# Seven products for more of the first MLP layer, and an own order for each chunk, in a fused attention and MLP kernel

## The chip, the cores and the metric

The kernel runs on one core of a Trainium2 chip. The metric is the device time of one execution in microseconds; the kernel before has a median of 330.25 us over three runs (330.21 to 332.17). The engines are called as the profile calls them: PE (TensorE, matmul), PEld (its weight loads), DVE (VectorE), ACT (ScalarE), POOL (GpSimd) and SP (SyncE, which issues DMAs). Each engine works through its own queue in program order; semaphores order the queues among themselves.

## The reference, cut to what matters

Attention with a forgetting gate over 8 batches, 8 heads, 576 positions and head size 64, and then an MLP of two layers with a tanh GELU over all 4608 rows.

```python
scores = scale * np.matmul(q, k.transpose(0, 1, 3, 2))
log_f = np.log(np.clip(f, 0.0001, 1.0))
cum = np.cumsum(log_f, axis=-1)
decay = cum[:, :, :, None] - cum[:, :, None, :]
scores = np.where(causal, -1000000000.0, scores + decay)
attn = np.exp(scores - max)          # then divided by its row sum
attn_out = np.matmul(attn, v)        # (8, 8, 576, 64)
x = attn_out.transpose(0, 2, 1, 3).reshape(4608, 512)
h = x @ w_in                         # 512 -> 2048
g = gelu_tanh(h)
out = g @ w_out                      # 2048 -> 512, float32
```

## The kernel before, in words

The 64 pairs of batch and head are worked in 16 "quads" of four heads. The 4608 rows of the MLP are worked in 9 "chunks" of 512 rows (0 to 8). The attention of a quad runs while an MLP chunk runs: chunk c is played together with the attention of the quads 2c+2, 2c+3 and the first part of 2c+4.

The order is written out by hand in tables of words. `SETUP` and `FRONT` are the first part of the program, up to chunk 1; `TABLES[c]` (from line 87) is the order within chunk c from chunk 2 on. `play(c)` goes through the words and calls the function behind each, and every function issues its instructions to the engines' queues at once. So a table sets, for each engine, the order of its queue. `q3` in a table means quad 2c+3, and so on. The words that matter here:

- `P.pr` (`mlp_in`, L369 and L376): one pair of 128 hidden features in full: 8 matmuls of 512 columns into one tile of PSUM, then one GELU of 1024 elements a partition on ACT. `P.pr.1` uses the tile `psO` of the attention, the others one of the two tiles of `psS`. Eight pairs make a chunk's first layer.
- `R.k` (`seven_in`, from L407): unit k, which stands for the pairs k and 4+k, in seven products of half size instead of eight (28 matmuls of 256 columns). It is called three times (R, R, R), which issue five products, one and one. It uses both `psS` tiles and both `psM` banks. Per unit DVE does one copy out of PSUM (L432) and five additions (L423), each with one operand in PSUM, and ACT does four GELUs of 512 elements (L428). Before, only the chunks 7 and 8 use it, for the units 1 and 3.
- `T` (`x_sums`, L390): four subtractions of 128x512 bf16 on DVE, both operands in SBUF, that make t1, t2, t4, t3 out of the next chunk's x; `R` multiplies with them. `K.k.n` (`w_sums`, L405): the same kind of sums of the weights for unit k, four in all, made once. Their results lie in the columns of x (`xT`) of a chunk that is done with (`HOMES`).
- `F.n`, `f.n` (`seven_products`, L504): the next n matmuls of the chunk's second layer, itself in seven products of 16 matmuls of 256 columns; `f` issues each as four matmuls of 32 columns of the array. After matmul 16 and 48 ACT copies a result (L525); after 32, 64, 80, 96 and 112 DVE adds (L529). `O.512` issues what is left of the chunk before.
- `G.half.which` (`gelu_sums`, L483 to L489): sums of the GELU's results for those seven products, 128x1024 bf16 on DVE, both operands in SBUF. Two of them (3 and 4 of half 1) are always issued after matmul 32.
- `S.i.r` (L256, L264): scores of quad i, round r, and their exponentials, two of 1024 elements a partition on ACT. They need both tiles of `psS`. `M.i.r` (L270): the causal mask on them, `affine_select` on POOL. `D.i` (L324, L343 to L347): row sums and their reciprocals on DVE. `V.i.x` (L324, L355): half of attention times v into `psO`, and DVE's product with the reciprocals into `xT`.
- `VW.i` (L210): v times the gate's weights, 128x1280, on POOL, both operands in SBUF. `CL.i` (L215): a small copy of it on DVE.
- `TK.i`, `TQ.i` (L193): transposes of k and q on DVE. `LK.i`, `LQ.i` (L187): their loads, issued by POOL. `LV` (L164): the load of v for the batch after next, issued by SP.
- `X`, `Y` (L224, L228): a tiny activation that makes ACT load the table for Exp or for GELU.

PSUM is full: `psS` has two tiles of two banks, `psM` two of one, `psO` one of two.

The few lines on which the steps rest:

```python
# line 387: t1, t2, t4, t3 of x, in this order
todo = ((t1, b12, b11), (t2, b22, t1), (t4, b21, t2), (t3, b22, b12))
# line 430: the first call of a unit
multiply(pa, a11, b11, True)      # then DVE copies pa
multiply(pb, s2, t2, True)        # each next one: DVE adds
multiply(pc, s1, t1, True)
multiply(pd, s3, t3, True)
multiply(pa, a12, b21, False)
```

Of the kernel before, what the change touches and what calls it, by code (L numbers as in the profile page):

```python
# [16 lines left out]
def kernel(  # L17
# [53 lines left out]
    """  # L71

    FRONT = """
        TQ.0 B.2.256 TK.1 SB TR LP.2@LQ.0 B.2.128 CW S.0.0 B.5.384 B.1.256 Z TQ.1 vw.0.0 S.0.2 WI.0 LQ.2 M.0.0 B.3.384 H.1.0.1
        LP.3 B.1.256 vw.1.0 WI.1@LU.4 W H.1.1.1 WI.3 B.2.256 WI.2 H.1.0.0 M.1.0.1 D.0.0 M.1.0.0 H.0.1.1 V.0.0.0 H.0.1.0 B.2.256 M.0.1 H.1.1.0 V.0.1.0
        D.1.0 H.0.3.0 B.2.128 V.1.0.0 LX.1.1 H.0.3.1 V.1.1.0 m.0.3.2 H.1.3.0 m.0.3.4 B.1.256 VW.1.1 H.1.3.1 B.4.128 vw.0.1 D.0.1 M.1.3 S.1.2 M.1.1 LK.2
        V.0.1.1 V.0.0.1 WO.0 J.0.1 D.1.1 J.0.0 WO.1@LV.1.1 V.1.1.1 V.1.0.1 J.0.3 WO.2@WI.1 VW.3 J.1.0 WO.3 LK.3 LQ.3 J.1.1 TQ.2 J.1.3 LQ.4
        LX.1.0@WO.2 TK.2 J.0.2 J.1.2 X LK.4 F.0.6 TK.3 B.3.256 S.2.0 LK.5 F.0.9 S.2.2 F.0.10 S.2.1 TQ.3 TQ.4 F.0.10 LV.2.0@LK.5 m.2.1 vw.2
        TK.4 S.3.0 f.0.1 M.2.2 CL.2 LQ.5 M.2.0 D.2 f.0.6 S.3.1 m.3.0 F.0.6 V.2.0 S.3.2 TK.5 LK.6 M.3.2 f.0.7 V.2.1 CL.3
        S.4.1 m.3.1 LQ.6 F.0.6 TQ.5 H.4.2.1 D.3 H.4.0.1 LQ.7 VW.4 H.4.0.0 V.3.1 v.3.0 f.0.3 H.4.2.0 CL.4 I.1.0 m.4.1 U.0 LV.2.1@LQ.5 I.1.4  # L80
        TQ.6 m.4.2.3 I.1.1 I.1.5 U.1 LV.3.0@LQ.7 m.4.2.2 TK.6 G.0 M.4.0 I.1.2 I.1.3 U.3 I.1.6 I.1.7 G.1.1.2 U.2 X F.1.14 S.5.0 f.1.28 S.5.1 D.4 M.5.0 f.1.16
        S.5.2 V.4.0 m.5.2.3 f.1.10 VW.5 V.4.1 CL.5 m.5.2.2 LQ.8 S.6.0 f.1.10 M.5.1 D.5 f.1.7 S.6.1 V.5.1 f.1.12 V.5.0 vw.6 S.6.2
# [39 lines left out]
    def many(n, shape, dtype, name):  # L122
        return [singles.tile(shape, dtype, name=f"{name}{i}") for i in range(n)]
# [11 lines left out]
    vw = many(2, [128, NT + 1, 4, D], BF16, "vw")  # L135
# [256 lines left out]
    def w_blocks(k):

        n = 256
        a11, a12, a21, a22 = (w_in_sb[:, 2 * b:2 * b + 2, HU * a + n * k:HU * a + n * (k + 1)]
                              for a in range(2) for b in range(2))
        old = xT[:, :, CH * HOMES[k]:CH * (HOMES[k] + 1)]
        return a11, a12, a21, a22, old[:, 0:2, 0:n], old[:, 0:2, n:], old[:, 2:4, 0:n]

    def w_sums(k, eng, which):  # L400

        a11, a12, a21, a22, s1, s2, s4 = w_blocks(k)
        todo = ((s1, a21, a22), (s2, s1, a11), (s4, a12, s2), (a21, a11, a21))
        for n in which or range(4):
            (eng.tensor_sub if n else eng.tensor_add)(*todo[n])  # L405

    def seven_in(c, k):  # L407

        a11, a12, s3, a22, s1, s2, s4 = w_blocks(k)
        b11, b12, b21, b22, t1, t2, t3, t4 = x_blocks(c)  # L410
        pa, pb = (psS.tile([128, 2, 512], FP32, name="ps_ab", tag="s")[:, 0].rearrange("p (j n) -> p j n", j=2) for _ in range(2))
        pc, pd = (psM.tile([128, 2, HC], FP32, name="ps_cd", tag="m") for _ in range(2))

        def multiply(ps, w, x, first):
            for j in range(2):
                for dt in range(2):
                    nc.tensor.matmul(ps[:, j], w[:, dt, 128 * j:128 * j + 128], x[:, dt],  # L417
                                     start=(first and j == 0 and dt == 0), stop=(dt == 1),
                                     skip_group_check=True)

        def add(ps, y, pool, tag):
            st = pool.tile([128, 2, HC], FP32, name="h_st", tag=tag)
            nc.vector.tensor_add(st, ps, y)  # L423
# [8 lines left out]
        nc.vector.tensor_copy(p1, pa)  # L432
# [226 lines left out]
    def load_values(b, half):  # L659
# [58 lines left out]
    def quads(call):  # L718
# [61 lines left out]
```

## Time and profile before

| | |
|---|---|
| median of three runs | 330.25 us |
| profiled execution: its span, the one time given of it | 328.4 us |
| median less that span | 1.85 us |
| PE busy | 316.9 us (96%) |
| DVE busy | 206.4 us (63%) |
| ACT busy | 201.7 us (61%) |
| POOL busy | 110.6 us (34%) |
| first `P` of chunk 2, 3, 4, 5 on PE at | 102.26, 137.11, 171.59, 206.06 us |
| first `P` of chunk 6, 7, 8 on PE at | 240.54, 273.40, 299.14 us |

All times in a view of the trace are microseconds from the start of the span. A row of the timeline gives the start, the time that the merged instructions took, the engine, the line, the operation, what it writes and reads, and how many were merged; in brackets stands how long the engine was idle before and who ended that. PE was granted its full clock throughout (1.00 in every stretch asked for).

A full 512-column matmul is shown with 379 ns, but that is from its issue to its modelled end; matmuls overlap. The 64 of a chunk's first layer fill 13.82 us, so one takes 0.216 us of PE.

### The profile page before, as it was taken

How to read it: one execution, taken by the hardware profiler on the slowest of the kernel's cores; microseconds unless marked ns; L12 is line 12 of the kernel's file. 1: busy time of each engine (PE TensorE's matmuls, PEld its weight loads, DVE VectorE, ACT ScalarE, POOL GpSimd, SP SyncE). 2: the span in 40 equal slices, each digit the busy share in tenths (PEclk: the TensorE clock that was granted, in tenths of full speed). 3: DMA queues.
4: the chain of work that ended last, by engine and by line, in shares of the span. 5: the costliest groups of instructions: out<-in, count | busy, mean ns of one | idle time of the engine just before them, and what ended most of it. 6: DMA issues, size and time to landing. Idle time of an engine off the chain costs nothing.

```text
span 328.4 us, 11961 instructions
## 1 busy us (share of the span) xinstructions
PE 316.9 (96%) x5421; PEld 206.5 (63%) x5421; DVE 206.4 (63%) x323; ACT 201.7 (61%) x231; POOL 110.6 (34%) x155
## 2 busy tenths in 40 slices
PE   3999999999999999999999999999999999999995
PEld 1458844545776477646774577557754777787684
DVE  4686039884887865674567456636553767875772
ACT  4685576866767586668656775768675841721630
POOL 8985572510504415520544054303440140000000
PEclk9999999999999999999999999999999999999999
DMA  7999999861124990295129711761110102002012
GB/s 123 210 214 215 168 230 199 167 165 24 36 40 94 236 208 31 94 187 108 37 68 182 140 37 36 160 122 36 36 66 0 36 21 81 2 32 98 0 35 96
DMA packets 44323, 33.42 MB, mean 102 GB/s; under 512 B 27488, under 2 KB 37856, under 8 KB 44272
## 3 DMA queue, kind: packets, MB, share of 16 engines
q0 software_dynamic: 8848, 16.58, 28.0%
q1 hardware_dynamic: 35280, 16.01, 18.4%
q8 instruction: 42, 0.69, 0.9%
q14 instruction: 9, 0.07, 0.1%
q10 hardware_dynamic: 144, 0.07, 0.1%
HBM read 36.85 MB, written 9.44 MB: 141 GB/s over the span
## 4 chain that ended last, share of the span: by engine, by line
PE 86%; DMA 3%; DVE 3%; ACT 3%; POOL 2%; issue 2%; POOLq 0%; DVEq 0%; ACTq 0%
PE ps_h L369 29%; PE ps_w L504 25%; PE po L324 9%; PE ps_s L256 8%; PE pso L574 4%; PE ps_h L458 4%; DMA v_nat<-in_v_dram 2%; PE ps_cd L417 2%; ACT pt L264 2%; PE ps_ab L417 2%; PE po_m L310 1%; POOL vw L210 1%; DMA out_dram<-o_st 1%; POOL v_nat L164 0%; PE ps_o L324 0%
## 5 line engine op out<-in xcount | busy, mean ns | idle before, releaser
L264 ACT ACTIVATE pt<-ps_s 128x1024 bf16<-128x1024 f32 (+2 forms) x100 | 93.7, 988 | 39.4 <-PE ps_s L256 34.9
L369 PE MATMUL ps_h<-xT,w_in_sb 128*128 128x512 bf16 x448 | 99.0, 379 | 0.0
L376 ACT ACTIVATE gT<-ps_h 128x1024 bf16<-128x1024 f32 x56 | 57.2, 1022 | 49.9 <-PE ps_h L369 48.3
L270 POOL TENSOR_SCALAR_AFFINE_SELECT pt<-pt 128x512 bf16<-128x512 bf16 (+3 forms) x65 | 38.2, 597 | 132.9 <-ACT pt L264 131.8
L369 PEld LDWEIGHTS <-w_in_sb 128*128 128x128 bf16 x448 | 43.8, 98 | 50.1 <-issue 0.4
L504 PEld LDWEIGHTS <-gT 128*32 128x32 bf16 (+1 forms) x1253 | 50.9, 97 | 6.4 <-issue 1.7
L504 PE MATMUL ps_w<-w_out_sb,gT 128*32 128x256 bf16 (+1 forms) x1056 | 46.9, 273 | 0.0
L504 PEld LDWEIGHTS <-gsum 128*32 128x32 bf16 (+1 forms) x1256 | 38.9, 97 | 2.7 <-issue 1.4
L256 PE MATMUL ps_s<-qT,kT 32*128 32x64 bf16 (+5 forms) x896 | 36.8, 263 | 0.3 <-ACT pt L264 0.2
L483 DVE TENSOR_TENSOR gsum<-gT 128x1024 bf16<-128x1024 bf16 x16 | 11.0, 689 | 35.2 <-ACT gT L376 35.2
L504 PE MATMUL ps_w<-usum,gsum 128*32 128x256 bf16 (+1 forms) x832 | 30.7, 273 | 1.0 <-ACT snap L525 0.7
L355 DVE TENSOR_TENSOR xT<-po,rb 128x576 bf16<-128x576 f32 x26 | 19.6, 755 | 18.9 <-PE po L324 18.6
L193 DVE STREAM_TRANSPOSE kT<-k_c 128x576 f32<-128x576 f32 x16 | 20.0, 1247 | 17.8 <-DMA k_c<-in_k_dram 17.8
L210 POOL TENSOR_TENSOR vw<-v_nat,wT 128x1280 bf16<-128x1280 f32 (+1 forms) x13 | 30.4, 2338 | 0.1
L529 DVE TENSOR_TENSOR o_st<-ps_w,snap 128x512 f32<-128x512 f32 x31 | 21.3, 689 | 13.2 <-PE ps_w L504 11.8
L256 PEld LDWEIGHTS <-kT 32*128 32x128 bf16 x896 | 16.9, 93 | 17.4 <-issue 12.6
L324 PE MATMUL po<-pt,vw 128*32 128x64 bf16 (+4 forms) x624 | 22.5, 279 | 0.0
L324 PEld LDWEIGHTS <-vw 128*32 128x32 bf16 x672 | 14.3, 96 | 10.6 <-issue 3.7
L193 DVE STREAM_TRANSPOSE qT<-q_c 128x576 f32<-128x576 f32 x16 | 19.9, 1242 | 1.1 <-PE ps_s L256 0.5
L164 POOL DMA_DIRECT2D v_nat<-in_v_dram x20 | 15.3, 776 | 4.6 <-DMA w_out_sb<-in_moe_w_out_dram 4.6
L504 PE MATMUL ps_w<-usum,gT 128*128 128x256 bf16 (+1 forms) x197 | 16.4, 273 | 0.0
L574 PE MATMUL pso<-w_out_sb,gT 128*32 128x512 bf16 (+1 forms) x115 | 15.6, 380 | 0.0
(97 smaller groups left out, 327.0 us busy)
## 6 DMA issues: line engine op xcount, KB each, us to landing
out_dram<-o_st SPq DMA_DIRECT2D x35, 256.0 KB, 2.4
k_c<-in_k_dram POOLq DMA_DIRECT2D x16, 288.0 KB, 5.8
q_c<-in_q_dram POOLq DMA_DIRECT2D x16, 288.0 KB, 7.3
v_nat<-in_v_dram SPq DMA_DIRECT2D x16, 256.0 KB, 8.5
w_in_sb<-in_moe_w_in_dram POOLq DMA_DIRECT2D x4, 512.0 KB, 9.5
w_out_sb<-in_moe_w_out_dram POOLq DMA_DIRECT2D x4, 512.0 KB, 8.3
v_nat<-in_v_dram SPq DMA_DIRECT2D x16, 128.0 KB, 3.5
v_nat<-in_v_dram POOLq DMA_DIRECT2D x13, 128.0 KB, 6.9
```

The lines of the kernel that those rows point to most:

```text
L193: nc.vector.transpose(out=dst.rearrange("p s c -> p (s c)").bitcast(FP32) .rearrange("p (t a) -> p a t", a=S // 32), in_=src.rearrange("p ...
L210: eng.tensor_mul(vw[i % 2][:, t0:t1], vb[:, t0:t1, h0:h0 + 4, :], wT[:, i, t0:t1, :].unsqueeze(3).to_broadcast([128, t1 - t0, 4, D]))
L256: nc.tensor.matmul(tiles[h // 2][:, h % 2, c0:c0 + nq], key_columns(i, key, h, c), qq[32 * h:32 * h + 32, q0:q0 + nq, c], start=(c == 0 an ...
L264: nc.scalar.activation(p[:, 2 * g:2 * g + 2, off:off + n], t[:, :, 0:n], AF.Exp, scale=scale)
L270: nc.gpsimd.affine_select(out=x, in_=x, compare_op=ALU.is_ge, fill=0.0, base=0, pattern=pattern, channel_multiplier=-1)
L324: nc.tensor.matmul(po[r0:r0 + w.shape[-1], 448 + q0:448 + q0 + nq], w, p[:, h, col:col + nq], start=(key in (0, "low")), stop=(key in ("lo ...
L355: nc.vector.tensor_mul(xT[:, 2 * u + x, S * b + s0:S * b + s1], po, rbs[i, part])
L369: nc.tensor.matmul(ph[:, j, :], w_in_sb[:, dt, 128 * ft:128 * ft + 128], xT[:, dt, CH * c:CH * (c + 1)], start=(dt == 0), stop=(dt == N_DT ...
L376: nc.scalar.activation(gT[:, 2 * pr:2 * pr + 2, :], ph, AF.Gelu_apprx_tanh)
L504: nc.tensor.matmul(ps[c0:c0 + width, n, cols[0]:cols[1]], x[:, j, 128 * n + c0:128 * n + c0 + width], w[:, j, cols[0]:cols[1]], start=(fir ...
L529: nc.vector.tensor_add(st, ps, kept[name])
L574: nc.tensor.matmul(pso[c0:c0 + cols, :], gT[:, ft, 128 * n + c0:128 * n + c0 + cols], w_out_sb[:, ft, :], start=(ft == 0), stop=(ft == N_F ...
```

## The change

Chunk 2 gets unit 1 in seven products, the chunks 3 to 6 the units 1 and 3 (as 7 and 8 had). The subtractions of x are no longer done at the end of the chunk before (`T`) but in the chunk itself (a new word, `TT`). The weight sums of unit 1 move from chunk 3 (and 6) into `FRONT`, for which `FRONT` gets the word `K`; those of unit 3 move from chunk 4 (and 6) into chunk 2. And each chunk from 2 to 8 has an order of its own: transposes and loads of q and k move from the start of the chunk to places behind it, `VW.q3` moves from the middle of a chunk to its start or into its first layer, `G`, `X`, `Y`, `CL`, `LV` and the masks have new places, and the second layer's matmuls are cut into other pieces between the attention's. The sum of these pieces stays 100 of the 112, with the rest in the next chunk's `O.512`; in chunk 6 it is 102. In `FRONT` nothing else changes: `K.1.0` stands behind the last but three `f` of quad 5's part, `K.1.1` after `V.5.1`, `K.1.2 K.1.3` after `S.6.2`.

```diff
     FRONT = """
...
-        S.5.2 V.4.0 m.5.2.3 f.1.10 VW.5 V.4.1 CL.5 m.5.2.2 LQ.8 S.6.0 f.1.10 M.5.1 D.5 f.1.7 S.6.1 V.5.1 f.1.12 V.5.0 vw.6 S.6.2
-        m.6.1 M.6.2.2 m.6.0 m.6.2.3 LK.7 LK.8 CL.6 LX.3.1@LK.6
+        S.5.2 V.4.0 m.5.2.3 f.1.10 K.1.0 VW.5 V.4.1 CL.5 m.5.2.2 LQ.8 S.6.0 f.1.10
+        M.5.1 D.5 f.1.7 S.6.1 V.5.1 K.1.1 f.1.12 V.5.0 vw.6 S.6.2 K.1.2 K.1.3 m.6.1 M.6.2.2 m.6.0 m.6.2.3 LK.7 LK.8 CL.6 LX.3.1@LK.6
...
-    TABLES.update(dict.fromkeys((2, 5), """
-        Y O.512 P.0 P.1 TK.q3 TQ.q3 LK.q5 LQ.q5 TK.q4 TQ.q4 LK.q6 LQ.q6 LV P.4 P.5 G.0 P.2 P.3 P.6 P.7 G.1.1.2 X F.10 S.q3.0
-        D.q2 M.q3.0 f.22 S.q3.1 V.q2.0 M.q3.1 VW.q3 f.18 S.q3.2 V.q2.1 M.q3.2 CL.q3 f.16 S.q4.0 D.q3 M.q4.0 f.18 S.q4.1 V.q3.0
-        M.q4.1 VW.q4 f.9 V.q3.1 f.7 S.q4.2 M.q4.2 CL.q4
-    """))
-    TABLES.update(dict.fromkeys((3,), """
-        Y O.512 P.0 P.1 TK.q3 TQ.q3 LK.q5 LQ.q5 TK.q4 TQ.q4 LK.q6 LQ.q6 LV K.1.0 K.1.1 K.1.2 P.4 P.5 G.0 P.2 P.3 P.6 P.7 G.1.1.2
...
-    TABLES.update(dict.fromkeys((6,), """
-        Y O.512 P.0 P.1 TK.q3 TQ.q3 LK.q5 LQ.q5 LV P.4 P.5 G.0 P.2 P.3 P.6 P.7 G.1.1.2 X F.10 S.q3.0 D.q2 M.q3.0 f.22 S.q3.1
-        V.q2.0 M.q3.1 VW.q3 f.18 S.q3.2 V.q2.1 M.q3.2 CL.q3 f.16 D.q3 f.18 V.q3.0 v.q3.1 T K.1.3 K.3.3 f.18
-    """))
-    TABLES.update(dict.fromkeys((7,), """
-        Y O.512 P.0.1 R.1 P.4.1 R.1 R.1 R.3 P.2.1 R.3 G.0.1.2 P.6 R.3 G.0.3.4 G.1.1.2 T
-    """))
-    TABLES.update(dict.fromkeys((8,), """
-        O.512 P.0.1 R.1 P.4.1 R.1 R.1 R.3 P.2.1 R.3 G.0.1.2 P.6 R.3 G.0.3.4 G.1.1.2
-    """))
+    TABLES[2] = """
+        VW.q3 O.512 P.3 TQ.q3 LQ.q5 P.7 P.0.1 TT R.1 K.3.0 P.4.1 TQ.q4 TK.q4 P.2 LV R.1 TK.q3 P.6 R.1 G.0 Y X G.1.1.2 CL.q3 LK.q5 D.q2 f.10 S.q3.0
+        M.q3.0 f.13 f.6 f.3 S.q3.1 f.12 V.q2.0 S.q3.2 f.4 V.q2.1 TQ.q5 f.2 f.11 f.2 TK.q5 f.3 M.q3.1 S.q4.0 M.q3.2 D.q3 f.12 f.2 V.q3.0 S.q4.1 VW.q4
+        LQ.q7 f.2 M.q4.0 f.2 V.q3.1 LQ.q6 K.3.1 K.3.3 f.9 f.7 S.q4.2 K.3.2 LK.q6 M.q4.1 M.q4.2 CL.q4 LK.q7
+    """
+    TABLES[3] = """
+        Y O.512 TT P.0.1 R.1 P.4.1 R.1 R.1 LV R.3 P.2.1 G.0.1.2 R.3 TQ.q4 P.6 R.3 VW.q3 G.1.1.2 F.7 S.q3.0 D.q2 f.3 f.22 S.q3.1 M.q3.1 M.q3.0 V.q2.1
+        f.12 f.5 G.0.3.4 TK.q4 S.q3.2 M.q3.2 TK.q5 V.q2.0 f.1 VW.q4 f.4 f.12 LK.q6 TQ.q5 LQ.q6 CL.q3 CL.q4 f.8 S.q4.0 M.q4.0 D.q3 f.8 f.2 f.6 S.q4.1
+        V.q3.0 f.3 LK.q7 f.7 X M.q4.1 V.q3.1 S.q4.2 M.q4.2 LQ.q7
+    """
+    TABLES[4] = """
+        TT Y O.512 P.0.1 R.1 P.4.1 R.1 R.1 LV R.3 VW.q3 P.2.1 TK.q4 R.3 P.6 TQ.q4 R.3 X F.10 S.q3.0 G.0.1.2 M.q3.0 CL.q3 G.1.1.2 D.q2 f.22 S.q3.1
+        V.q2.0 G.0.3.4 M.q3.1 f.12 S.q3.2 M.q3.2 TK.q5 V.q2.1 VW.q4 f.6 f.5 f.10 S.q4.0 D.q3 f.1 f.9 V.q3.0 LQ.q6 M.q4.0 S.q4.1 f.2 M.q4.1 LK.q7 f.4
+        f.3 f.8 f.1 f.7 V.q3.1 S.q4.2 LK.q6 M.q4.2 TQ.q5 LQ.q7 CL.q4
+    """
+    TABLES[5] = """
+        Y VW.q3 O.512 P.0.1 TT R.1 P.4.1 R.1 R.1 R.3 LV G.0.1.2 G.0.3.4 P.2.1 P.6 R.3 R.3 TQ.q4 D.q2 S.q3.0 f.9 G.1.1.2 f.1 f.22 S.q3.1 V.q2.0 M.q3.1
+        TK.q4 LK.q6 f.14 S.q3.2 TQ.q5 LQ.q6 f.4 M.q3.0 M.q3.2 V.q2.1 VW.q4 f.9 S.q4.0 f.1 CL.q3 TK.q5 f.5 X f.1 D.q3 f.7 f.7 f.4 f.1 V.q3.1 LK.q7 LQ.q7
+        M.q4.0 S.q4.1 M.q4.1 f.3 f.5 V.q3.0 f.7 S.q4.2 M.q4.2 CL.q4
+    """
+    TABLES[6] = """
+        Y O.512 TT P.0.1 R.1 P.4.1 R.1 R.1 LV R.3 G.0.1.2 P.2.1 R.3 VW.q3 P.6 R.3 G.0.3.4 F.1 X F.9 S.q3.0 D.q2 f.7 M.q3.0 G.1.1.2 f.7 f.2 V.q2.0
+        S.q3.1 M.q3.1 f.6 f.1 f.15 S.q3.2 M.q3.2 f.2 f.9 CL.q3 V.q2.1 f.7 f.16 D.q3 v.q3.1 f.3 f.3 f.5 f.6 f.3 V.q3.0
+    """
+    TABLES[7] = """
+        Y O.512 TT P.0.1 R.1 P.4.1 R.1 R.1 R.3 P.2.1 G.0.1.2 R.3 R.3 P.6 G.1.1.2 G.0.3.4
+    """
+    TABLES[8] = """
+        O.512 TT P.0.1 R.1 P.4.1 R.1 R.1 R.3 P.2.1 R.3 R.3 G.0.1.2 G.0.3.4 P.6 G.1.1.2
+    """
...
+        "K": lambda k, *which: w_sums(k, nc.vector, which),
...
+        "TT": lambda c, *which: x_sums(c, which or range(4), nc.vector),
```

## The prediction, as put on record

> **What bounds the kernel now.** I read the page's busy times first, then who waited for whom on PE.
>
> ```profile
> span 328.4 us, 11961 instructions
> PE 316.9 (96%) x5421; PEld 206.5 (63%) x5421; DVE 206.4 (63%) x323; ACT 201.7 (61%) x231; POOL 110.6 (34%) x155
> PEclk9999999999999999999999999999999999999999
> ```
>
> ```profile
> PE ps_lt L607 <- ACT f_sb L602: 4.8, 1, 4.8
> PE cum_ps L634 <- POOL before L627: 1.0, 1, 1.0
> PE ps_w L504 <- ACT snap L525: 0.7, 1, 0.7
> ```
>
> PE is busy from 6 us to the end, and in all it waits for another engine for 7.5 us, 4.8 of them at the start. The busy share alone would not prove it, since matmuls overlap; from start to start one of 512 columns takes 0.216 us (the 64 of a chunk's first layer: 13.82 us) and one of 256 columns 0.109 us, so columns set the pace. Then the stretches of the chunks 5, 6 and 7 (length; busy time and instructions of PE, PEld, DVE, ACT, POOL; clock):
>
> ```profile
> 206.00:240.50 34.50, 34.50 (x705) 22.18 (x703) 19.96 (x29) 23.63 (x27) 11.63 (x15) 1.00 0.38 85
> 240.50:273.40 32.90, 32.63 (x654) 21.47 (x653) 19.24 (x33) 20.09 (x23) 6.49 (x9) 1.00 0.10 33
> 273.40:299.10 25.70, 25.37 (x202) 19.54 (x200) 18.57 (x31) 9.68 (x14) 0.00 (x0) 1.00 0.13 41
> ```
>
> PE fills its stretches; DVE is at 58% in chunk 5. In chunk 7, which already has two units in seven products, the timeline of the first layer:
>
> ```profile
> 273.40 1.89 PE L369 MATMUL ps_h<-xT,w_in_sb 128*128 128x512 bf16 x8
> 275.13 0.60 PE L417 MATMUL ps_ab<-xT,w_in_sb 128*128 128x256 bf16 x4
> 275.77 0.69 DVE L432 COPY snap<-ps_ab 128x512 f32<-128x512 f32 x1 [1.09 <-PE ps_ab L417]
> 276.56 0.69 DVE L423 TENSOR_TENSOR h_st<-ps_ab,snap 128x512 f32<-128x512 f32 x1
> 277.31 1.89 PE L369 MATMUL ps_h<-xT,w_in_sb 128*128 128x512 bf16 x8
> ```
>
> A pair takes 1.73 us to the next start (273.40 to 275.13). DVE follows a unit's products by 0.6 us, one operation of 0.69 each.
>
> **What it saves.** A unit in full is 16 x 0.216 = 3.45 us, in seven products 28 x 0.109 = 3.06. Check: chunk 7's first layer runs from 273.40 to 286.43, 13.03 us against 13.82, so 0.395 a unit. Nine units are added (chunk 2 one, chunks 3 to 6 two each): -3.55 us on PE.
>
> **What it adds beside PE.** Per unit DVE gets six operations of 0.69 (4.15 us), and in chunks 2 to 6 `TT`, four of 0.42 (L390), 1.68 us. In chunk 5 DVE goes from 19.96 of 34.5 us to 29.9 of 33.7, 89%. ACT gets four GELUs of 0.62 for two of 1.02, 0.4 a unit: small.
>
> **What waits it gives back.** Look at chunk 6, where PE has a wait it just doesn't see:
>
> ```profile
> 255.60 1.28 ACT L224 ACT_TABLE_LOAD   x1
> 257.00 1.90 ACT L264 ACTIVATE pt<-ps_s 128x1024 bf16<-128x1024 f32 x2
> 259.45 0.63 PE L256 MATMUL ps_s<-qT,kT 32*128 32x64 bf16 x16
> ```
>
> Seen from the first `P` (240.54), the exponentials of `S.q3.0` end at 18.36 and `S.q3.1`, which needs their PSUM, starts at 18.91. With 0.8 us less of first layer PE comes at 18.1, but ACT's chain isn't earlier. In chunks 3 and 4 the last addition of unit 3 stands behind a transpose on DVE (`TQ.q4`, 1.25, ends 13.9; in chunk 5 behind four `G`, in chunk 2 behind `TK.q3`): addition to 14.6, GELU to 15.2, table 1.28, exponentials 1.94: 18.45. So 0.1 to 0.6 is lost again in each of the five chunks, 1.6 together. DVE's full queue adds to it. In chunk 2 it has, from 13.75 on, without a gap: the unit's last addition, `G.0` and `G.1.1.2` (six of 0.66), `CL`, `D`'s chain (1.9), the addition after matmul 32, two more `G` and `V.q2.0`'s product, to 23.4; PE is ready for `V.q2.1`, which needs `psO` back, at 22.5. Walking the other chunks the same way I come to 0.7 (3), 0.75 (4), 0.6 (5), 0.35 (6) and 1.6 (2), 4.0 in all with the 1.6 in it. Between the bounds 1.6 and 4.0 I take 2.8, since my walk lets DVE's operations touch, where the trace lets some overlap by 0.06.
>
> **What old waits it removes.** 0.53 at 266.79 in chunk 6 (`D` for a mask; `D.q3` now stands farther behind it), 0.5 at 292.16 in chunk 7 (a product for an addition that stood behind `T` and `G` on DVE; `T` is gone), 0.35 at 125.12 in chunk 2 (scores for their PSUM). -1.35; at worst 0.
>
> **Two operands in SBUF.** This decides the sign. One row of before has a maximum four times its median (min/median/max), and the timeline shows why:
>
> ```profile
> L489 DVE TENSOR_TENSOR gsum<-gT,gsum x16: 684/685/2823, 77.2 to 317.1; 128x1024 bf16<-128x1024 bf16 x16
> ```
>
> ```profile
> 86.47 0.68 DVE L487 TENSOR_TENSOR gT<-gT 128x1024 bf16<-128x1024 bf16 x1
> 86.64 2.71 POOL L210 TENSOR_TENSOR vw<-v_nat,wT 128x1280 bf16<-128x1280 f32 x1
> 87.06 2.82 DVE L489 TENSOR_TENSOR gsum<-gT,gsum 128x1024 bf16<-128x1024 bf16 x1
> ```
>
> A `G` on DVE, with both operands in SBUF, was started while POOL multiplied v, and it ended 0.5 us after POOL did: it stood still for 2.1 us. The `G` ahead of it, started first, made POOL's 2.33 into 2.71. So the two exclude each other, whoever comes first goes, and a waiting POOL gets in between two back-to-back operations of DVE. A mask does the same (a product by `causal`, L299, took 0.855 for 0.42 over a mask at 102.77). An addition from PSUM is not held, as chunk 5's start shows (0.68 inside the multiply at 203.73). [...]
>
> Now chunk 5's start in before:
>
> ```profile
> 203.73 2.33 POOL L210 TENSOR_TENSOR vw<-v_nat,wT 128x1280 bf16<-128x1280 f32 x1
> 204.21 0.68 DVE L529 TENSOR_TENSOR o_st<-ps_w,snap 128x512 f32<-128x512 f32 x1
> 206.06 6.21 PE L369 MATMUL ps_h<-xT,w_in_sb 128*128 128x512 bf16 x28
> 206.34 0.69 DVE L529 TENSOR_TENSOR o_st<-ps_w,snap 128x512 f32<-128x512 f32 x1
> 206.92 1.23 POOL L270 TENSOR_SCALAR_AFFINE_SELECT pt<-pt 128x512 bf16<-128x512 bf16 x2 [0.87 <-ACT pt L264]
> ```
>
> Count from `P` (206.06). The last masks of the chunk before run from 0.86 to 2.09 on POOL, the last addition on DVE from 0.28 to 0.97. In before DVE's next are transposes, which nothing holds (1.25, their median). After the change, in chunk 3, it is `TT`, from 0.95, into the masks; and POOL's next, behind a load's issue of 0.55, is `VW.q3`, which had stood behind `M.q3.1`. In turn: mask to 1.49, t1 to 1.9, mask to 2.53, t2 to 2.95, t4 to 3.37, `VW` to 5.7, t3 to 6.1. PE wants t2 at 2.17 (+0.85 of waiting) and then t3 at 3.9 (+2.25): 3.1 us. DVE's copy and additions for the unit stand behind t3, so nothing is caught up. Chunk 6 has no issue in between and comes to the same 3.1; in chunk 5 `TT` starts at 1.25 (behind `TQ.q5` and `CL`), the same again. Chunk 4 has `TT` ahead of `O`: from -1.0 to 0.7, before the masks; nothing. Chunk 2's `VW.q3` waits for v (landed at 114.57, 12.3 into the chunk), long behind its `TT`; 7 and 8 have no POOL work. So 3 x 3.1 = 9.3. Bounds: 0.85 each (2.55) if t3 slips in ahead of `VW`, and 0 if none of it meets. I take 9.3, since the one row that shows a POOL multiply against back-to-back `G` has POOL getting in.
>
> The same between `G` and masks: `G.1.3.4` in chunk 2, `G.0.3.4` in chunk 3, `G.1.1.2` in chunk 6, where exponentials end as they start: 0.6, 0.6 and 0.3 us of PE at most, 0 at least; 0.7 taken.
>
> **Moves at no cost.** `K` in `FRONT` and chunk 2: eight of 0.42 on DVE; around 92 to 100 us DVE waits 0.36, 0.75 and 0.19, and PE doesn't wait for it; 0 to 0.5. Behind chunk 2's waiting `VW.q3` on POOL stand `LQ.q5`, `LK.q5` and `M.q3.0`, used past 24 us into the chunk, 10 later. Loads of q and k land 5.8 and 7.3 us after issue (page), their transposes come over 10 later; DVE covers that. `LV` on SP, some 5 us later than before, lands 8.5 after issue, and `VW.q4` comes at about 23. Without `X` or `Y` ACT loads its table by itself as early (L376's load at 68.09 began 0.02 us after the work before it). Moved masks end over 1 us before their `D`. The new pieces of `f` have the same sum and as many changes between the shapes of matmul (12 a chunk, 2.2 us in chunk 5): +-0.2 a chunk.
>
> **The sum.** -3.55 - 1.35 + 2.8 + 9.3 + 0.7 = +7.9 us. The profiled span of 328.4 becomes 336.3; the median of the runs shown lies 1.85 above that span: 338.2. Its own range: if only half of two of the meetings counts (7.1), with waits of 1.6 and no `G`, +3.8, 334; with 4.0, 1.5 and 0.5 for `K`, +10.4, 341.
>
> **Rivals.** *Small meetings.* t3 goes before `VW` each time: -3.55 - 1.35 + 2.8 + 2.55 + 0.7 = +1.15, 331.4. For it: `VW` is ready at 3.05, only 0.3 us before t3's turn at 3.37. Against: the row at 87.06. *DVE is the bound, no lock.* -3.55 - 1.35 + 4.0 = -0.9, 329.4. For it: 89% busy; against: two rows show the lock. *Faster.* One mechanism: `TT` ends before POOL turns to masks and `VW`, in chunks 3, 5 and 6 as in 4, and only the exponentials hold PE, 0.5 to 1.6: -4.4 to -3.3, 326.3. It decides if the end of `TT` lies under 0.86 us after `P`; for it, chunk 4 is built so; against, `O`'s addition alone ends at 0.97. That the units don't save what they should is no rival: chunk 7 shows the 0.395.
>
> **Chances.** About 1% (3.3 us) is what a measurement of this kernel can tell from no change. My forecast 62%, all of it slower by over 1%; the small meetings 15% and DVE as the bound 10%, both within 1%: 25%; faster 13%. The range from 326.5 to 341 leaves out about half of the last case and the tail above, some 12%; with the sign as forecast it is 334 to 341.
>
> **What would show it.** Right: in chunks 3, 5 and 6 the subtractions at L390 take 0.42 in some rows and over 2 us in one, with POOL's L210 beside it, and PE waits at L417 for DVE L390; chunk 4 has none. First-layer products in all, L369 and L417, 13.0 us a chunk less those waits. Scores at L256 wait for ACT's L264. Wrong: L210 in those chunks starts after the last L390, or L390 keeps its 0.42 beside it; then the saving stands and 328 or less comes out.

## The result, and the profile after

The kernel after takes 340.6 us (median of four executions, 339.87 to 341.99), the kernel before 331.2 in the same comparison (330.21 to 334.41). The ratio is 1.030, with a 95% interval of 1.026 to 1.034: slower, as forecast, and 2.4 us above the forecast of 338.2. Of the 71 executions of the kernel before that were timed beside the experiments, five have a mean granted clock of 0.984 or 0.985 and take 333.5 to 334.5 us, and one execution each of e2, e5 and e11 below is of that kind; none of them was traced, so what lowers their clock is open. The page of the profiled execution (span 340.3 us, time 341.99), its first lines:

```profile
span 340.3 us, 12422 instructions
PE 318.6 (94%) x5578; PEld 219.1 (64%) x5598; DVE 259.1 (76%) x397; ACT 202.5 (60%) x249; POOL 113.2 (33%) x155
PEclk9999999999999999979999999899997999999999
```

DVE is busy for 52.7 us more: 37.4 for nine units (4.15 each), 8.4 for `TT` in five more chunks (1.68 each), and 7 more. That rest is a net figure: the rows of `TT` in the chunks 3, 5 and 6 alone are 8.9 us longer than 1.68 each. PE's share fell from 96 to 94%. New is the third line: before, the granted clock was shown as full in every slice; now a 7, an 8 and another 7 stand in it. The largest of PE's waits (us in total, times, longest), which before was the 4.8 at the start:

```profile
PE ps_cd L421 <- DVE xT L394: 6.8, 3, 2.5
```

All line numbers after the tables are four higher than before: L394 is the subtraction of x, L421 a unit's product, L214 `VW`, L274 the masks. Three waits of PE for L394 make 6.8 us. The row of L394 itself (min/median/max in ns):

```profile
L394 DVE TENSOR_TENSOR xT<-xT x28: 409/424/2964, 106.9 to 313.1; 128x512 bf16<-128x512 bf16 x28
```

One of 0.42 us took 2.96. The stretch of chunk 5 (length; busy time of PE, PEld, DVE, ACT, POOL; clock):

```profile
212.08:250.29 38.21, 35.67 (x757) 25.05 (x756) 32.35 (x47) 23.75 (x31) 11.12 (x13) 0.96 0.36 83
```

In chunk 5 PE is idle for 2.5 us of the stretch, where it had none, and its clock is 0.96 in the mean; in chunk 6 the same (2.2 us idle, 0.95). Where it happens is seen at the start of chunk 3 (first `P` at 140.00), in the timeline:

```profile
140.81 4.84 DVE L394 TENSOR_TENSOR xT<-xT 128x512 bf16<-128x512 bf16 x4
140.83 1.67 POOL L274 TENSOR_SCALAR_AFFINE_SELECT pt<-pt 128x512 bf16<-128x512 bf16 x2 [4.08 <-ACT pt L268]
...
143.02 2.34 POOL L214 TENSOR_TENSOR vw<-v_nat,wT 128x1280 bf16<-128x1280 f32 x1
...
145.72 0.61 PE L421 MATMUL ps_cd<-xT,w_in_sb 128*128 128x256 bf16 x4 [2.51 <-DVE xT L394]
...
147.12 3.19 PE L373 MATMUL ps_h<-xT,w_in_sb 128*128 128x512 bf16 x8
```

`TT` runs from 140.81 to 145.65, 4.84 us for four operations of 0.42, beside POOL's two masks and then its multiply, and PE stands idle for 2.51 us until the last of the four has ended. Here the fourth, t3, is the one that stands behind the multiply, and in chunk 6 too; in chunk 5 it is the third, t4 (2.85 us), and t3 follows it in 0.41. The last line holds what the forecast had not: a pair in full, 1.89 us elsewhere, takes 3.19 right behind that wait.

The lengths of all parts, from the first `P` or `R` of a chunk on PE to that of the next (an ordinary table; the last two columns are experiments told below):

| part | before | after | TT out of the way (c5_behind) | last version |
|---|---|---|---|---|
| up to chunk 2 | 102.26 | 102.70 | 102.61 | 102.73 |
| chunk 2 | 34.85 | 37.30 | 36.73 | 34.93 |
| chunk 3 | 34.48 | 38.51 | 34.02 | 34.00 |
| chunk 4 | 34.47 | 33.57 | 33.58 | 33.58 |
| chunk 5 | 34.48 | 38.21 | 33.76 | 33.76 |
| chunk 6 | 32.86 | 35.45 | 31.55 | 31.54 |
| chunk 7 | 25.74 | 25.47 | 25.24 | 25.46 |
| chunk 8 to the end | 29.3 | 29.1 | 29.4 | 29.1 |

The chunks 3, 5 and 6 lose 4.0, 3.7 and 2.6 us, chunk 2 loses 2.45, and the chunks 4 and 7 win 0.9 and 0.27. Chunk 4 is the one whose table has `TT` as its first word.

### The profile page after: what moved, and what is told of

Read it like the earlier page. It is cut to its first block, busy times and chain, and to the rows that moved or that the text cites. A ratio compares the mean times of both kernels' runs of the same rounds, so it can differ in the third digit from the quotient of the medians.

```text
span 340.3 us, 12422 instructions
## 1 busy us (share of the span) xinstructions
PE 318.6 (94%) x5578; PEld 219.1 (64%) x5598; DVE 259.1 (76%) x397; ACT 202.5 (60%) x249; POOL 113.2 (33%) x155
## 4 chain that ended last, share of the span: by engine, by line
PE 76%; DVE 13%; issue 4%; ACT 3%; POOL 2%; DMA 1%; DVEq 0%; POOLq 0%; ACTq 0%
PE ps_w L508 22%; PE ps_h L373 17%; PE ps_s L260 8%; PE po L328 7%; PE ps_cd L421 6%; PE ps_ab L421 4%; PE ps_h L462 4%; PE pso L578 4%; DVE xT L394 4%; ACT pt L268 2%; PE po_m L314 1%; DVE h_st L427 1%; DVE gT L491 1%; DVE o_st L533 1%; DVE xT L359 1%
## 5 line engine op out<-in xcount | busy, mean ns | idle before, releaser
L274 POOL TENSOR_SCALAR_AFFINE_SELECT pt<-pt 128x512 bf16<-128x512 bf16 (+3 forms) x65 | 40.8, 638 | 143.9 <-ACT pt L268 142.0
L373 PE MATMUL ps_h<-xT,w_in_sb 128*128 128x512 bf16 x288 | 72.2, 392 | 0.8
L380 ACT ACTIVATE gT<-ps_h 128x1024 bf16<-128x1024 f32 x38 | 38.6, 1019 | 40.2 <-PE ps_h L373 38.9
L373 PEld LDWEIGHTS <-w_in_sb 128*128 128x128 bf16 x304 | 30.6, 101 | 33.0 <-issue 4.5
L427 DVE TENSOR_TENSOR h_st<-ps_cd,h_st 128x512 f32<-128x512 f32 x52 | 35.1, 688 | 13.1 <-PE ps_cd L421 10.3
L214 POOL TENSOR_TENSOR vw<-v_nat,wT 128x1280 bf16<-128x1280 f32 (+1 forms) x13 | 30.6, 2354 | 6.8 <-DMA v_nat<-in_v_dram 6.7
L533 DVE TENSOR_TENSOR o_st<-ps_w,snap 128x512 f32<-128x512 f32 x31 | 21.2, 683 | 14.2 <-PE ps_w L508 11.5
L421 PEld LDWEIGHTS <-w_in_sb 128*128 128x128 bf16 x208 | 20.9, 102 | 13.1 <-DVE xT L394 7.6
L260 PEld LDWEIGHTS <-kT 32*128 32x128 bf16 x896 | 16.8, 93 | 17.6 <-issue 11.9
L359 DVE TENSOR_TENSOR xT<-po,rb 128x576 bf16<-128x576 f32 x26 | 19.5, 751 | 7.3 <-PE po L328 6.8
L432 ACT ACTIVATE gT<-h_st 128x512 bf16<-128x512 f32 x39 | 22.6, 623 | 1.7 <-DVE h_st L427 1.3
L421 PE MATMUL ps_cd<-xT,w_in_sb 128*128 128x256 bf16 x104 | 16.4, 283 | 6.8 <-DVE xT L394 6.8
L328 PEld LDWEIGHTS <-vw 128*32 128x32 bf16 x672 | 15.0, 97 | 10.9 <-issue 4.1
```

Of the source, the lines that this page charges most:

```text
L214: eng.tensor_mul(vw[i % 2][:, t0:t1], vb[:, t0:t1, h0:h0 + 4, :], wT[:, i, t0:t1, :].unsqueeze(3).to_broadcast([128, t1 - t0, 4, D]))
L260: nc.tensor.matmul(tiles[h // 2][:, h % 2, c0:c0 + nq], key_columns(i, key, h, c), qq[32 * h:32 * h + 32, q0:q0 + nq, c], start=(c == 0 an ...
L274: nc.gpsimd.affine_select(out=x, in_=x, compare_op=ALU.is_ge, fill=0.0, base=0, pattern=pattern, channel_multiplier=-1)
L328: nc.tensor.matmul(po[r0:r0 + w.shape[-1], 448 + q0:448 + q0 + nq], w, p[:, h, col:col + nq], start=(key in (0, "low")), stop=(key in ("lo ...
L373: nc.tensor.matmul(ph[:, j, :], w_in_sb[:, dt, 128 * ft:128 * ft + 128], xT[:, dt, CH * c:CH * (c + 1)], start=(dt == 0), stop=(dt == N_DT ...
L380: nc.scalar.activation(gT[:, 2 * pr:2 * pr + 2, :], ph, AF.Gelu_apprx_tanh)
```

## The experiments

(The names e1 to e12 number the experiments; each runs the kernel after with the edit shown, unless it says that it starts from the kernel before.) The theory: in chunks 3, 5 and 6 `TT` and POOL's masks and `VW` exclude each other (the "lock" of the prediction's rivals), PE waits 2.1 to 2.5 us for the last subtraction, and that idle time is what takes half the clock from the next 3.4 us. The rivals: that DVE is simply too full for the units; that the new orders themselves cost (loads and transposes that come later); that the clock falls for another reason than the wait.

**TT first** (e1). One word moved in three tables:

```diff
-        Y O.512 TT P.0.1 R.1
+        TT Y O.512 P.0.1 R.1
```

The same in chunk 6, and in chunk 5 `TT` from behind `P.0.1` to the front.

> The changed kernel with TT as the first word of chunks 3, 5 and 6, as chunk 4 has it; nothing else moves. Theory of the exclusion (a subtraction with both operands in SBUF stands still while POOL masks or multiplies): the subtractions run before POOL's masks, every L394 takes about 0.42 us, PE's three waits of 2.3 to 2.7 us go, and with them the three stretches of half clock of 3.4 us: 340.6 - 3 x (2.5 + 1.7) = about 328. Rival, DVE simply has too much to do (259 us busy): the same operations in nearly the same order, 338 to 341.

Measured: 332.74 us (331.42 to 333.24), ratio 1.006 (1.004 to 1.009). Chunk 3 is 34.0 and chunk 6 31.5, 4.5 and 3.9 less than after: there the theory holds. Chunk 5 still has 36.94, and the timeline around its start (first `P` at 206.93) shows why:

```profile
207.37 4.97 DVE L394 TENSOR_TENSOR xT<-xT 128x512 bf16<-128x512 bf16 x4
...
212.99 0.60 PE L421 MATMUL ps_cd<-xT,w_in_sb 128*128 128x256 bf16 x4 [2.87 <-DVE o_st L533]
```

Being first in the table of chunk 5 is not enough, since chunk 4 ends with a transpose and a copy on DVE (`TQ.q5`, `CL.q4`): `TT` starts 0.44 after `P` and meets the masks and `VW` (from 209.70) all the same. What PE waits for by the profile is the addition behind `TT` on DVE (L533), which frees the PSUM bank of the next product. So the time is 4.7 us above the expected 328. The first word of a table is not the first on its engine.

**TT out of the way in chunk 5 too** (e5). In addition, the last words of chunk 4 move behind `TT`:

```diff
-        f.3 f.8 f.1 f.7 V.q3.1 S.q4.2 LK.q6 M.q4.2 TQ.q5 LQ.q7 CL.q4
+        f.3 f.8 f.1 f.7 V.q3.1 S.q4.2 LK.q6 M.q4.2
...
-        Y VW.q3 O.512 P.0.1 TT R.1
+        TT Y O.512 TQ.q3 LQ.q5 CL.q2 VW.q3 P.0.1 R.1
```

> As e1_tt_first, and TQ.q5, LQ.q7 and CL.q4 at the end of chunk 4 go behind chunk 5's TT, which in e1 still met masks and multiply (2.9 us of waiting on PE, chunk 5 at 36.9 us). Exclusion: chunk 5 comes to about 33.7, the whole to 332 - 3.2 = about 329, with no clock stretch below 1.00 in any run. Rival, chunk 5 is long because DVE's queue is full there: 331 to 333.

Measured: 328.5 us (327.7 to 331.6), ratio 0.996 (0.994 to 0.999). Chunk 5 is 33.76. The clock is full in the profiled execution (1.00), but not "in any run": the one of 331.44 us has a mean clock of 0.984. Where `TT` stands, with the three words that went behind it, is worth the whole loss: 12 us from 340.6. In chunk 3 of this kernel (first `P` at 139.34):

```profile
137.98 1.68 DVE L394 TENSOR_TENSOR xT<-xT 128x512 bf16<-128x512 bf16 x4
...
140.17 1.22 POOL L274 TENSOR_SCALAR_AFFINE_SELECT pt<-pt 128x512 bf16<-128x512 bf16 x2 [3.68 <-ACT pt L268]
```

The same four subtractions take 1.68, and are through 0.5 us before POOL's first mask.

**VW behind the masks of the next round** (e2). The other side of the meeting is moved: `VW.q3` goes back behind `M.q3.1` in chunks 3, 5 and 6, `TT` stays.

> The changed kernel with VW.q3 of chunks 3, 5 and 6 put back behind M.q3.1, where the kernel before has it. Exclusion: the masks still meet the subtractions (0.3 to 0.9 us of waiting on PE a chunk, too short for the clock to fall), the multiply doesn't: 340.6 - 3 x (2.0 + 1.7) = about 329.5; up to 332 if the multiply now meets G sums later in the chunk. Rival, too much on DVE: POOL's multiply is of no account, 338 to 341.

Measured: 332.63 us (332.33 to 335.5), ratio 1.008 (1.005 to 1.010). With the masks alone `TT` takes 2.29 in chunk 3 instead of 4.84; PE starts its fourth product 0.12 late there, and in chunk 5 it waits 0.26 for the second subtraction. So the multiply, not the masks, was the costly half. The time is a little above the 332 that the expectation allowed for, since chunk 3 still has 36.34: at its new place (161.53) the multiply meets a `G` sum, which takes 2.82 us for 0.68, and behind it in DVE's queue a transpose and a product of `V` come late, for which PE waits 0.5 and 1.0.

**The wait filled with work** (e3, e10). To tell the clock from the wait, useless matmuls are put where PE would wait; they compute nothing that is used.

```diff
+        for _ in range(20 if k == 1 and c in (3, 5, 6) else 0):
+            nc.tensor.matmul(pd[:, 0], a11[:, 0, 0:128], b11[:, 0], start=True, stop=True,
+                             skip_group_check=True)
         multiply(pd, s3, t3, True)
```

e10 has 10 in place of 20.

> The changed kernel with 20 useless matmuls of 256 columns (2.2 us) ahead of the fourth product of unit 1 in chunks 3, 5 and 6, into the PSUM that this product then overwrites: PE has work while it would wait for t3, and the wait itself stays. If the half clock after each wait comes from PE standing idle: no stretch below 1.00, 340.6 - 3 x 1.7 = about 335.5. Rival, the clock falls for another reason (the load of the kernel as a whole): clock stretches stay, 340 to 341.

> As e3_filled with 10 useless matmuls instead of 20, 1.1 us of the wait filled, so that PE stands idle for about 1.2 to 1.6 us instead of 2.3 to 2.7. If the clock falls only after an idle time near 2.3 us, no stretch below 1.00 and the time of e3, 336; if any idle time over 1 us does it, the three stretches are back and it is 340.6. The kernel before had idle times of 0.9 at most and no such stretch.

Measured: 336.15 us with 20 (336.07 to 336.7; ratio 1.017, 1.014 to 1.020) and 336.2 with 10 (336.02 to 336.96; 1.018, 1.016 to 1.019). Both execute more matmuls than after and are 4.4 us faster. The page's clock row with 20, and then the waits with 10, whose clock row is the same:

```profile
PEclk9999999999999999999999999999999999999999
```

```profile
PE ps_cd L421 <- DVE xT L394: 3.5, 3, 1.4
```

`TT` is as slow as before (2.96 us for its longest), and the product starts as late; only PE isn't idle so long, and the clock stays full. So the half clock follows from the idle time, not from more work. In the two profiled executions the chunks 3, 5 and 6 are 1.7, 1.5 and 1.5 us shorter with 20 than in after, 4.7 in all; the medians differ by 4.4, in which chunk 2 may have a part (37.30 in after and 36.39 with 20, though its words are the same). Breaking the wait into idle stretches of at most 1.4 us does as well as filling it.

**The exclusion without a reader** (e4, e11). In the kernel before, `VW.q3` is moved to the start of chunks 3, 5 and 6 (e4), and then four unused subtractions are put behind `O.512` there (e11), so that DVE and POOL meet as in the change, but PE needs nothing of it.

> The kernel before with VW.q3 as the first word of chunks 3, 5 and 6, nothing else. Exclusion: DVE has transposes there, which read one operand, so nothing is held: 330 to 331.5, same. Rival, POOL's multiply at a chunk's start slows whatever DVE does: 2 us or more in each chunk, 336 or more.

> As e4_before_vw_early (the order of before with VW.q3 first in chunks 3, 5 and 6), with four subtractions of the kind of TT behind O.512 there, whose results nobody uses. Exclusion: they stand still beside masks and multiply as in the changed kernel (one L390 of over 2 us a chunk), but PE waits for none of them; DVE's transposes come about 5 us later and are still in time. 330 to 331.5. Rival, the blocked subtractions cost their time whoever needs them: 340.

Measured: 330.31 us (ratio 0.999, 0.997 to 1.001) and 330.45 (1.001, 0.999 to 1.003). Timeline of e11 at chunk 3:

```profile
138.26 4.43 DVE L395 TENSOR_TENSOR xT<-xT 128x512 bf16<-128x512 bf16 x4
...
139.92 2.49 POOL L215 TENSOR_TENSOR vw<-v_nat,wT 128x1280 bf16<-128x1280 f32 x1
```

The same 4.4 us for 1.7, and no time lost. Here the exclusion as such is free; it costs where PE waits for the operation that is held.

**The orders without the units, the units without the orders** (e7, e8). e7 has the new tables, with the pairs in full in chunks 2 to 6 in place of `R` and without `TT`; e8 has the old tables, with `R` put into the first layer, the four transposes left there, and the subtractions at the end of the chunk before (`T`), in chunk 2 as `TT`. The weight sums stand in chunk 6 in e7, in `FRONT` and chunk 2 in e8.

> The orders of the changed kernel without its added units: P for R in chunks 2 to 6, no TT there, all weight sums in chunk 6. Exclusion: no subtraction stands where POOL multiplies, so none of the three waits and no half clock; chunks 3 to 6 at the length of before (34.5, 34.5, 34.5, 32.9 or a little less), chunk 2 up to 1.5 longer by its order: 330 to 332. Rival, the order itself (POOL's multiply early, transposes late) is what slows: 335 or more.

> The added units in the order of before: R for P, four transposes still in the first layer, T behind V.q3.1 at the chunk's end, weight sums in FRONT and chunk 2. If the units need an order that takes transposes out of the first layer: DVE ends the transposes about 10.4 us into a chunk, R.3 needs an addition behind them at 7.4, so 3 us and more of waiting a chunk in 3, 4 and 5, each long enough for a stretch of half clock (1.7): 340 to 350. Rival, the units are worth their 3.5 us in any order: 327.

Measured: e7 332.42 us (331.7 to 333.35; ratio 1.005, 1.000 to 1.010), e8 367.43 (366.35 to 368.03; 1.112, 1.109 to 1.115). The new orders cost about 2 us by themselves (by the interval, 0 to 3.3), so the units' gain is to be read against e7: to e5 it is 3.9 us, and 3.7 over the chunks 3 to 6, 0.46 a unit; e5 differs from e7 in the place of a few other words too, so the 0.46 is not the units' alone. In the old order the units cost 37 us, far more than I had expected. Its largest waits:

```profile
PE ps_cd L412 <- DVE h_st L418: 10.8, 4, 3.2
PE ps_ab L412 <- DVE snap L427: 9.9, 4, 2.9
```

Transposes of 1.25 stand between a unit's additions; with 2.3 for L524 PE waits 23 us for DVE. The mean clock of 0.947 over a span of 366.3 us is another 19 at most, less where PE was idle at half clock too. My expectation had counted one stretch of half clock in each of the chunks 3 to 5, 5.1 us in all; by an estimate from that mean, 19 us are eleven stretches of 1.7.

**Chunk 2 as before** (e6, e9, e12). What is left of the loss is chunk 2, 36.73 in e5 against 34.85. All three take e5 and give chunk 2 its old order without a unit, with the weight sums, transposes and loads that the new order of chunk 3 needs (`CL.q4` moves into chunk 3, and `TT` stays that table's first word). The edit, cut:

```diff
-        VW.q3 O.512 P.3 TQ.q3 LQ.q5 P.7 P.0.1 TT R.1 K.3.0 P.4.1 TQ.q4 TK.q4 P.2 LV R.1 TK.q3 P.6 R.1 G.0 Y X G.1.1.2 CL.q3 LK.q5 D.q2 f.10 S.q3.0
...
+        Y O.512 P.0 P.1 TK.q3 TQ.q3 LK.q5 LQ.q5 TK.q4 TQ.q4 LK.q6 LQ.q6 LV P.4 P.5 G.0 P.2 P.3 P.6 P.7 G.1.1.2 X F.10 S.q3.0
...
+        M.q4.1 K.3.0 K.3.1 f.9 V.q3.1 K.3.2 K.3.3 f.7 S.q4.2 M.q4.2
```

They differ in one word, the fourth weight sum `K.1.3`, which changes a block of the weights in place. In e6 it stays in `FRONT`, so chunk 2's first layer multiplies with the changed block and its results are not the reference's: its time shows only what the order costs. In e9 it leaves `FRONT` for the end of chunk 2:

```diff
-        M.q4.1 K.3.0 K.3.1 f.9 V.q3.1 K.3.2 K.3.3 f.7 S.q4.2 M.q4.2
+        M.q4.1 K.3.0 K.3.1 f.9 V.q3.1 K.3.2 K.3.3 K.1.3 f.7 S.q4.2 M.q4.2
```

In e12, instead, for the place right behind the first layer:

```diff
-        Y O.512 P.0 P.1 TK.q3 TQ.q3 LK.q5 LQ.q5 TK.q4 TQ.q4 LK.q6 LQ.q6 LV P.4 P.5 G.0 P.2 P.3 P.6 P.7 G.1.1.2 X F.10 S.q3.0
+        Y O.512 P.0 P.1 TK.q3 TQ.q3 LK.q5 LQ.q5 TK.q4 TQ.q4 LK.q6 LQ.q6 LV P.4 P.5 G.0 P.2 P.3 P.6 P.7 G.1.1.2 K.1.3 X F.10 S.q3.0
```

> As e5_c5_behind, and chunk 2 in the order of before without its unit (with the weight sums and the transposes that the later chunks need). If chunk 2's loss (36.4 us against 34.9 before, although it has 0.4 us less on PE) comes from its order: chunk 2 at about 34.9 to 35.2, the whole about 1.4 below e5, 327.5, faster than before. Rival, the weight sums and the two transposes for the next chunk cost it wherever they stand: as e5.

> As e6_c2_plain, with K.1.3, which changes a block of w_in in place, moved from FRONT behind chunk 2's full products, so that these use the weights as they are. One DVE operation of 0.42 us moves; nothing waits for it until chunk 3. 326.5, as e6, 1.1% under the kernel before.

> Of the changed order this keeps chunks 3 to 8 with their units, with TT as the first word of chunks 3, 5 and 6 and chunk 4's TQ, LQ and CL behind TT of chunk 5; chunk 2 has the order of before, without a unit, and the fourth first-layer subtraction of unit 1 (K.1.3) stands behind all eight products of chunk 2, right after its G sums, where no other word is near. The output is the reference's. Theory (the time is set by whether TT starts before POOL's masks and VW): chunk 2 ends on DVE as it did in the kernel that gave 326.49, TT of chunk 3 is through before the masks, chunk 3 takes 34.0, and the time is 326.5, ratio 0.989. Rival (the position of K.1.3 was not what cost e9 its 2.2 us in chunk 3, but the subtraction's work as such, as a chunk 2 that ends later on DVE): 328.5 to 329, chunk 3 at 35 to 36.

Measured: e6 326.49 us (326.42 to 327.43; ratio 0.989, 0.987 to 0.991), e9 329.05 (328.33 to 331.04; 0.997, 0.995 to 0.998), e12 326.7 (326.22 to 328.12; 0.986, 0.980 to 0.992, beside 330.58 for before). e9 missed, by one subtraction of 0.42. Its timeline at chunk 3 (first `P` at 137.12):

```profile
139.57 2.32 POOL L214 TENSOR_TENSOR vw<-v_nat,wT 128x1280 bf16<-128x1280 f32 x1
...
139.73 2.24 DVE L219 COPY vw<-vw 64x256 bf16<-64x256 bf16 x1
...
142.75 0.60 PE L421 MATMUL ps_ab<-xT,w_in_sb 128*128 128x256 bf16 x4 [2.00 <-DVE snap L436]
```

`TT` started 0.12 ahead of `P` (in e12 0.45), met a mask and ended 1.98 behind it (1.22); with the addition that follows, the small copy `CL` then came 0.16 us after `VW` had started, and took 2.24 us, for 0.22 elsewhere. The unit's copy stood behind it, and PE waited 2.00. In e12 `TT` is through before the masks and `CL` starts 0.43 before `VW`; its row of L394 has nothing over 0.43:

```profile
L394 DVE TENSOR_TENSOR xT<-xT x24: 412/424/426, 137.2 to 297.8; 128x512 bf16<-128x512 bf16 x24
```

e12 keeps eight of the nine units and is 3.9 us faster than the kernel before, and chunk 3 has the 34.0 that was expected.

## Why the prediction was right in sign and short in size, step by step

The step that failed is the price of a wait. The sum lets each meeting cost the time that PE waits, "3 x 3.1 = 9.3", and puts the clock at nothing without a reason; the runs show a window of half clock behind each of the three waits, 5.1 us in the profiled execution. Besides, two terms were mis-sized: the chunks 3 to 6 without the meetings (-3.4 for -1.6) and chunk 2 (+2.45 for +0.7).

The spans differ by 11.9 us, where the sum had 7.9; the profiled execution of after is the slowest of the four, and the medians differ by 9.4 (by 10.35 from the 330.25 on which the forecast stood). By its terms, with its 2.8 for new waits and its 0.7 for the `G` sums divided over the chunks as it had walked them:

| term of the sum | forecast | measured | from |
|---|---|---|---|
| meetings of `TT` with masks and `VW` | +9.3 | +7.7 | start-to-start of PE in chunks 3, 5, 6 of after: 2.68, 2.34 and 0.42, 2.26 |
| half clock behind the three waits | none | +5.1 | three stretches of 3.413 us at 0.50 |
| units, old waits, new waits, `G`, chunks 3 to 6 | -1.6 | -3.4 | chunks 3 to 6 of e5 against before |
| the same in chunk 2 | +0.7 | +2.45 | table of lengths |
| up to chunk 2, chunks 7 and 8 | -0.5 | -0.05 | table of lengths |

That the total came so near is in part luck: the meetings were put 1.6 too high and the saving of the chunks 3 to 6 1.8 too low, which hides nearly half of what was missing.

**The step "Two operands in SBUF" held in kind.** Long rows of L394 in chunks 3, 5 and 6, with L214 beside them, none in chunk 4; PE waiting at L421 for L394; POOL getting in between two operations of DVE. Its size was 3.1 us a meeting and came out at 2.3 to 2.8. The part that failed is "PE wants t2 at 2.17 (+0.85 of waiting)": the masks delayed each of the first subtractions by 0.3 only (0.74 us for 0.42), so t2 was there in time in chunks 3 and 6 and 0.42 late in chunk 5, 0.26 of it idle. The wait for t3, forecast as 2.25, was 2.68, 2.34 and 2.26 from start to start, of which PE was idle for 2.51, 2.17 and 2.10.

**The missing term is the clock.** The sum let a wait cost its own length. The windows of 3.413 us around the waits in chunks 3 and 6 of after (length; PE's busy time; clock):

```profile
142.92:146.33 3.41, 0.90 (x8) 1.00 1.11 200
146.33:149.74 3.41, 3.41 (x11) 0.50 1.06 222
...
252.14:255.56 3.42, 1.35 (x13) 1.00 0.22 74
255.56:258.97 3.41, 3.39 (x12) 0.50 0.00 0
```

After each of the waits one whole window runs at half the clock, which costs half of 3.413 us, 1.7. Three times makes 5.1 in the profiled execution; the three others have a mean clock of 0.988 to 0.990 instead of 0.985, so about two of three. e3 and e10 take just this away and give back 4.4 by the medians, 4.7 in the three chunks. The page of before had shown a clock of 1.00 throughout, and I took it as given. But its record of the clock starts only 12.5 us into the span, and the rows ahead of that time speak for half the clock there: of the useless matmuls of 384 columns that the kernel issues there (L235), six from 10.54 on (the last of them smaller) take 1.99 us, three from 12.86 on 0.66; one by one they start every 0.32 us and then every 0.16. From there on PE is hardly idle in before, and that trace shows no half clock.

**Given-back waits.** The walk along DVE's queue gave up to 2.4 us in chunks 3 to 6. In e5, where nothing meets, these chunks take 132.91 us, and before less eight units of 0.395 and the old wait of 0.53 would be 132.60: so 0.3 for the given-back waits and the `G` meetings together. There even the lower bound, 0.1 to 0.6 a chunk for the exponentials, was not reached. Chunk 2 went the other way: forecast 1.6 at most for the waits and 0.6 for `G`, found 2.3 (e1, e2, e3) to 3.2 (after) over the 34.1 that its work asks for. Part is as the prediction had it, `V.q2.1` waiting for the product of `V.q2.0`, which stands in DVE's full queue. Two lines of after:

```profile
125.74 0.74 DVE L359 TENSOR_TENSOR xT<-po,rb 128x576 bf16<-128x576 f32 x1
126.54 0.87 PE L328 MATMUL po<-pt,vw 128*32 128x512 bf16 x24 [0.40 <-DVE xT L359]
```

PE starts `V.q2.1` right after L359, which started when a `G` sum (L493, to 125.82) let it. A hole of 0.80 in `V.q2.0`, at 123.94, has no releaser in the trace, but costs nothing of its own: in e2 and e3 it isn't there, and the wait for L359 is 1.6 and 1.4 instead. A second one, 1.02 in `S.q4.2` of after and 0.6 in e5, is absent in e2 and e3; what makes it stays open. The words up to the end of chunk 2 are the same in after, e1, e2, e3, e5 and e10, and chunk 2 takes 36.1 to 37.3 us in their profiled executions; so about 1 us of its +2.45 can't be put down to the order.

**The old waits** went away in chunk 6 as forecast (31.54 is 32.86 less 0.53 and two units). In chunk 7 0.27 was gained instead of 0.5, while six of the other kernels gain the 0.5 (25.24); chunk 2 gained nothing.

**The rivals.** *Small meetings* is out: t3 never came ahead of `VW`, and in chunk 5 even t4 stood behind it. *DVE is the bound* is out for chunks 3 to 6: in e12, whose chunk 5 is that of e5, DVE is busy for 30.2 of its 33.76 us, and PE for 33.65. *Faster* named the right condition, `TT` through before POOL turns to masks and `VW`, and a time of 326.3 for it. e5, which fulfils it in all three chunks with all nine units, has 328.5, since chunk 2 takes 36.73; e12, which leaves chunk 2 alone and so is no longer the kernel that was forecast, has 326.7.

## What to carry to other kernels

Price a wait on PE by what it does to the clock as well: 2.3 to 2.8 us of waiting cost four or more here, and useless matmuls in the gap were worth 4.4 us of 340. When an order is searched or written, the place of an operation is not its word in the list but what its engine still has to do when its operands are there; one more operation of 0.42 us cost 2.4 us that way. An operation of DVE that reads two operands from SBUF belonged here before POOL's work (four of `TT` took 1.68 us there in e5, 4.84 beside masks and `VW` in after), or where nobody waits for it (4.43 in e11, with no time lost).

## What the chip showed that was not expected

**The clock goes by windows.** The three half-clock stretches of after start at 146.33, 218.01 and 255.56, and the gaps between them are whole multiples of 3.413 us (71.68 is 21 and 37.55 is 11 of them), so these three lie on one grid. In steps of that length, from the start of the clock's record to the last matmul, the windows of after in which PE was busy for 0.90, 1.17 and 1.35 us were each followed by one at half clock; no other one of after (2.39 and more) was, and none of before (2.75 and more, and 1.52 in the one with its last matmuls). Two near the bound, one of e8 and one of e1 (in e1 PE was idle for 2.87 us, but that wait lay across two windows):

```profile
115.90:119.31 3.41, 1.55 (x13) 0.80 (x12) 3.17 (x6) 2.96 (x4) 0.53 (x1) 1.00 1.16 228
119.31:122.73 3.42, 3.42 (x69) 1.93 (x72) 2.44 (x4) 3.38 (x5) 0.00 (x0) 0.50 0.94 176
```

```profile
211.26:214.67 3.41, 1.68 (x11) 1.06 (x11) 3.20 (x5) 0.45 (x1) 0.79 (x1) 1.00 0.47 111
214.67:218.09 3.42, 3.42 (x28) 2.58 (x27) 2.85 (x5) 2.29 (x5) 0.00 (x0) 1.00 1.19 235
```

So a bound near 45% of a window (between 1.52 and 1.55 us of 3.41) fits these executions, and a wait can cost 1.7 us more or nothing, by where it falls (2.87 us in e1 cost nothing more in its profiled execution, 2.10 in chunk 6 of after cost the 1.7). The executions without a trace fit that: in e1, four of eight have a mean clock of 0.995 (1.7 us less of full clock), the rest 0.997 to 1.0; in e9, with its wait of 2.00, four of twelve have 0.993 or 0.994 and take 330.3 to 331.0 us, the rest 328.3 to 329.2.

**A copy with one operand is held too.** `CL`, 64x256 bf16 from SBUF to SBUF, took 2.24 us beside `VW` (e9, the row above) for its usual 0.22, and 0.54 in e12, where it began while a mask still ran. The prediction had the exclusion for operations with two SBUF operands only; a transpose, which also reads one, kept its 1.22 us inside `VW` (e2, at 168.19). What sets the copy apart no run shows.
